# Fused Fourier mixing and MLP on one core: lighter warm-up products, a new first pair of products, and rows, weights and sums taken in another order

## The chip, the core and the metric

The kernel runs on one core of a Trainium2 chip. Its time is the device time of one execution in microseconds (us); the median of three runs of the kernel before is 850.76 us (850.23 to 850.90). Engines are named as the profile names them: PE (matrix products; PEld is its weight load), DVE (vector), ACT (scalar functions), POOL (GpSimd), SP (here a queue that only issues DMAs). POOL and ACT issue DMAs as well.

## What is computed

For x of 2048 rows and 640 columns:

```python
xn = layernorm(x)                       # no scale, no shift
a = xn @ dft_hid_re.T ; b = xn @ dft_hid_im.T
y = dft_seq_re @ a - dft_seq_im @ b     # Fourier mixing, real part
h = gelu_tanh(xn @ w1 + b1)             # 640 -> 1536
out = x + y + h @ w2 + b2               # 1536 -> 640
```

Everything is float32. The inputs hold the four DFT matrices in full (two of 2048 by 2048, two of 640 by 640).

## The kernel before

**Arithmetic.** A float32 operand is kept as a pair: a high part (written by ACT as a copy rounded to fp32r) and a low part (DVE: operand minus high part). A product of two operands is three PE instructions, high by high, high by low, low by high (`product`, L278 to L280; in the first MLP layer L304). `split` (L160 and L161) makes a pair. Nearly all PE instructions have 128 by 128 weights and 512 moving columns.

**Stages.** The 2048 rows are four blocks t of 512. Blocks 0 and 1 go through the MLP as written: iteration i of 12 takes 128 hidden units, and is one `hidden` (15 products), one `gelu` and one `output` (15 products into five banks). Blocks 2 and 3 are computed with fewer products from sums and differences of blocks and weights (`head`, `mid`, `finish`). Then come the two Fourier products, from 190 us on, which the change doesn't touch.

**The front (0 to 21 us).** Block 0 is four chunks of 128 rows. SP and ACT load one chunk each in turn. Before the rows arrive, PE runs ten products of zeros into a bank (`warm_up`, L676); their operand is a 128 by 512 tile that DVE clears (L665) and casts (L667). DVE (L185, L705) or ACT (L699 for the sum, L716) centers each chunk, PE transposes it by products with an identity matrix (`transpose_x`, L693, float32, 128 columns each), and `split` makes the pairs XT[j] from the five banks. W1[0] is split in two parts (L728, L729). Then `hidden(0)` and `hidden(1)` (L304) run as two blocks of 15, and `hidden(2)` follows, with four transposes (L764) after its first product. Scaling by the row's deviation is applied later (RB).

**Block 1's iterations (t = 1, i = 0 to 11, 95 to 178 us).** The program order of one iteration is: `hidden(g+2)`, `gelu(g+2)`, `output(g)`, `second_block(i)`, then `prep_w` of one step. So the pair `hs` that `gelu` makes in iteration i (ACT L322, ACT L326, DVE L328) is used by PE in iteration i+2. `second_block(i)` prepares blocks 2 and 3: mean and variance of chunks 12 to 15 (`ln_stats`, L185), their scaling (`ln_scale`, L192 to L197, with a change of ACT's function table; `ln_apply`, L201) and writing back to DRAM (`xs`, 16 DMAs, eight on POOL, eight on SP, L203), then reading block 2 and block 3 back turned by rows (`load_z`, L234) and turning them on DVE (`turn_z2`, `turn_z1`, L786 and L792). One buffer ("zo") holds, one after the other, block 0's result, block 2's rows, block 3's rows and block 1's input.

`prep_w` makes the weight pairs of the two 640 by 640 DFT matrices (wr and wi). Step s is column group j = s // 3 and part k = s % 3: k = 0 turns two raw tiles on DVE (L396) and loads the next two, and each part splits what it makes into regions of one staging tile `wst` and sends them to DRAM (`wits`, L418, POOL's queue). A region is written again only after its DMA has landed, and ACT, which runs its instructions in order, waits there with everything behind it.

**The end of block 1 (172 to 191 us).** `outs` and `outs_at` add the bias on ACT (L368), transpose a bank on DVE (L371) and add the rows on POOL (L373). `forms_ob` (sums of rows, the split of w1's sums TW[1], and one form) stands between two of them. A product that opens a bank (in `head(1)`: banks 5 and 6) waits until DVE has transposed what the bank held.

Queues run in program order; there is no scheduler. Tiles of one place wait for each other by tile.

Of the kernel before, what the change touches and what calls it, by code (L numbers as in the profile page):

```python
# [15 lines left out]
P = 128  # L16
Q = 4
B = 32
EPS = 1e-5
NWARM = 10  # L20
TAIL = 4
# [5 lines left out]
def kernel(  # L27
# [78 lines left out]
    def bank(k):  # L106
        return banks[:, k]
# [179 lines left out]
    def unit(g):  # L287
        return g if g < NF else LATE[g % NF]

    def hidden(g, aside=None):  # L290
# [4 lines left out]
        if g == 0:  # L295
            steps = FIRST
        if g == 1:

            steps.sort(key=lambda s: s[1] == 2)
        for n, (j, k) in enumerate(steps):  # L300
            if aside and n == ASIDE:
                aside()
            a, b = kinds[k]
            nc.tensor.matmul(  # L304
                acc, W1[i][:, a, j * P : (j + 1) * P], XT[j][:, b], start=n == 0, stop=n == len(steps) - 1
            )
        return acc


    FIRST = [(0, 0), (0, 2), (1, 0), (1, 2), (0, 1), (2, 0), (2, 2), (1, 1), (3, 0), (3, 2)]  # L310
    FIRST += [(2, 1), (4, 0), (4, 2), (3, 1), (4, 1)]

# [351 lines left out]
    make_identity(nc, ident)  # L664
    nc.vector.memset(zeros, 0.0)  # L665
    warm = whole["as"][:, :TB]
    nc.vector.tensor_copy(warm, zeros)  # L667

    nc.scalar.activation(eps[:, 1:2], eps[:, 0:1], AF.Sqrt)
    load_w1(0, cuts=(0, 2, ND))  # L670
    load_w1(1, cuts=(0, 2, ND))

    wacc = bank(0)

    def warm_up():
        nc.tensor.matmul(wacc, warm[:, :P], warm, start=True, stop=True)  # L676

    for k in range(NWARM):
        warm_up()
    load_w1(2)  # L680
    load_w2(0)
# [39 lines left out]
    ln_stats(2)  # L721
    center(2, ALU.subtract, MV[:, 2, 0:1])
    sum_on_act(3)
    center(3, ALU.add, MV[:, 3, 5:6], 0, 2)
    center(3, ALU.add, MV[:, 3, 5:6], 2, ND)
    for lo, hi in ((0, 2 * P), (2 * P, D)):
        h, l = (W1[0][:, k, lo:hi] for k in range(2))
        nc.scalar.activation(h, first_w1[:, lo:hi], AF.Copy)  # L728
        nc.vector.tensor_tensor(l, first_w1[:, lo:hi], h.bitcast(F32), op=ALU.subtract)  # L729
    transpose_x(0, 0, ND)  # L730
# [11 lines left out]
    acc0 = hidden(0)  # L742
    prep_w1(1)
    acc1 = hidden(1)

# [59 lines left out]
    def sums_w1(q):  # L805
# [7 lines left out]
        add(r[:, 2:4, :P], r[:, 2:4, :P], r[:, 2:4, P:], ALU.subtract)  # L813

    def split_w1(q):
        if q >= NF // 2:
            return
        TW[q] = A["tw"].tile([P, 2, 8 * P], F32R, tag=f"tw{q % 2}", bufs=1, name=f"tw{q}")
        split(TW[q][:, 0], TW[q][:, 1], RQ.pop(q).rearrange("p a b -> p (a b)"))
        TW[q] = TW[q].rearrange("p a (c f) -> p a c f", c=4)  # L820
# [149 lines left out]
    def open_tw():  # L970
        A["es"].close()
        A["w"] = None
        A["es"] = ExitStack()
        A["tw"] = pool("twp", stack=A["es"])

    def open_xf():
        es_rows.close()
        A["esx"] = ExitStack()
        A["xf"] = pool("xfp", side="right", stack=A["esx"])
        A["xfx"] = A["xf"].tile([P, 2, 2, TB], F32R, name="xfx")  # L980
        A["fifth"] = A["xf"].tile([P, TB], F32, name="fifth")
        load_rq(0)
# [66 lines left out]

    w_early = {0: (0,), 1: (1,), 2: (2,), 3: (3,), 4: (4,), 5: (5,)}  # L1050
    prep_w1(3)
    gelu(1, acc1)
    for g in range(NG):
# [37 lines left out]
        elif i < NF - 2:  # L1091
# [3 lines left out]
            second_block(i)  # L1095
            for k in w_early.get(i, ()):
                prep_w(k)
        elif i == NF - 2:
# [43 lines left out]

    outs(1, (0,), yt=lambda n: AB[:, 0], done=False)
    forms_ob()
    outs_at((2, 1), (4, 5))
    mid(0, rest)
# [659 lines left out]
```

## Time and profile before

| | us |
|---|---|
| median of three runs | 850.76 |
| the profiled execution: its own time | 853.42 |
| the profiled execution: span from the first to the last instruction | 851.6 |
| PE busy in the span | 842.5 |
| DVE, ACT, POOL busy in the span | 668.0, 355.3, 53.6 |
| first product of the first layer starts | 9.66 |

How to read it: PE is busy for 99% of the span, so what counts is where it isn't fed, and the share of any other engine over the whole span says little. A matmul's recorded duration (389 ns for 512 columns) is longer than the distance between two of them (227 ns), so a gap between two starts tells more than idle time. In a row of the timeline stand the start, the duration, the engine, the line, the operation, out<-in, the shapes and the count; in brackets stands the idle time before it and what ended it.

### The profile page before, as it was taken

The page shows a single profiled execution, that of the slowest core. Times are in us where ns is not written, and L with a number is a line of the kernel's source. Part 1 is how long each engine was busy: PE and PEld are TensorE (multiplying, and loading weights), DVE is VectorE, ACT ScalarE, POOL GpSimd, SP SyncE. Part 2 cuts the span into 40 slices and gives each one's busy share as a digit, 9 for nine tenths or more (in the row PEclk, how much of TensorE's full clock was granted, in tenths as well). Part 3 has the DMA queues.
Part 4 walks back from the last instruction along what each step waited for, and adds up shares of the span by engine and source line. Part 5 has one row for each costly group of instructions (what it writes and reads, how often), then busy time and mean ns, then how long its engine had stood idle before and what let it go on. Part 6 is the DMA issues. An engine that isn't in the chain of part 4 may idle for free.

```text
span 851.6 us, 10345 instructions
## 1 busy us (share of the span) xinstructions
PE 842.5 (99%) x3707; PEld 694.5 (82%) x3707; DVE 668.0 (78%) x841; ACT 355.3 (42%) x499; POOL 53.6 (6%) x78
## 2 busy tenths in 40 slices
PE   8999999999999999999999999999999999999997
PEld 6888888778888888888888888888888888888886
DVE  6766764795757888879988787899977898885687
ACT  7454533555655554333434343232322423223241
POOL 0000313131221300000000000000000000000001
PEclk9999999999999999999999999999999999999999
DMA  6667799738669998948743669763865879805464
GB/s 185 187 185 186 162 215 252 196 79 195 207 216 347 360 218 158 188 102 204 164 137 95 177 211 285 171 139 97 213 164 171 253 184 228 312 18 179 124 170 108
DMA packets 207363, 158.45 MB, mean 186 GB/s; under 512 B 81040, under 2 KB 180880, under 8 KB 206800
## 3 DMA queue, kind: packets, MB, share of 16 engines
q1 hardware_dynamic: 198368, 134.59, 62.2%
q0 software_dynamic: 4400, 21.89, 6.5%
q10 hardware_dynamic: 4544, 1.31, 0.6%
q8 instruction: 29, 0.48, 0.2%
q14 instruction: 22, 0.18, 0.1%
HBM read 114.76 MB, written 42.99 MB: 185 GB/s over the span
## 4 chain that ended last, share of the span: by engine, by line
PE 83%; DVE 4%; DMA 4%; ACT 3%; issue 3%; SPq 2%; POOL 1%; ACTq 0%; POOLq 0%; DVEq 0%
PE banks L278 27%; PE banks L279 26%; PE banks L280 26%; PE banks L304 3%; DMA x<-in_A_x_dram 1%; DMA wit<-wst 1%; SPq L388 1%; DMA xs<-x 1%; ACT ab L322 1%; SPq L203 0%; SPq L178 0%; POOL wit L418 0%; DVE r L161 0%; ACT hs L326 0%; DVE tw L161 0%
## 5 line engine op out<-in xcount | busy, mean ns | idle before, releaser
L278 PE MATMUL banks<-as,xab 128*128 128x512 f32 x411 | 160.0, 389 | 0.6 <-DVE zs L371 0.6
L279 PE MATMUL banks<-as,xab 128*128 128x512 f32 x411 | 159.9, 389 | 0.0
L280 PE MATMUL banks<-as,xab 128*128 128x512 f32 x411 | 159.9, 389 | 0.0
L160 ACT ACTIVATE as<-r 128x1024 fp32r<-128x1024 f32 x80 | 85.0, 1062 | 177.9 <-PE banks L280 149.5
L161 DVE TENSOR_TENSOR as<-r,as 128x1024 fp32r<-128x1024 f32 x80 | 97.1, 1215 | 41.5 <-ACT as L160 41.5
L278 PEld LDWEIGHTS banks<-as,xab 128*128 128x128 f32 x411 | 77.2, 188 | 17.0 <-DVE zs L371 1.0
L279 PEld LDWEIGHTS banks<-as,xab 128*128 128x128 f32 x411 | 77.2, 188 | 16.0
L280 PEld LDWEIGHTS banks<-as,xab 128*128 128x128 f32 x411 | 77.2, 188 | 15.9
L278 PE MATMUL banks<-as,xc 128*128 128x512 f32 x224 | 87.1, 389 | 0.0
L279 PE MATMUL banks<-as,xc 128*128 128x512 f32 x224 | 87.1, 389 | 0.0
L280 PE MATMUL banks<-as,xc 128*128 128x512 f32 x224 | 87.1, 389 | 0.0
L160 ACT ACTIVATE as<-rt 128x1024 fp32r<-128x1024 f32 x32 | 34.0, 1063 | 70.5 <-PE banks L280 62.5
L304 PE MATMUL banks<-xtt,xab 128*128 128x512 f32 x240 | 57.2, 391 | 0.2 <-ACT xtt L160 0.2
L304 PEld LDWEIGHTS banks<-xtt,xab 128*128 128x128 f32 x240 | 44.7, 188 | 10.1 <-ACT xtt L160 0.6
L278 PEld LDWEIGHTS banks<-as,xc 128*128 128x128 f32 x224 | 42.1, 188 | 8.8
L280 PEld LDWEIGHTS banks<-as,xc 128*128 128x128 f32 x224 | 42.1, 188 | 8.7
L279 PEld LDWEIGHTS banks<-as,xc 128*128 128x128 f32 x224 | 42.0, 188 | 8.7
L161 DVE TENSOR_TENSOR as<-rt,as 128x1024 fp32r<-128x1024 f32 x32 | 38.8, 1211 | 5.3 <-ACT as L160 5.3
L160 ACT ACTIVATE as<-u 128x1024 fp32r<-128x1024 f32 (+1 forms) x24 | 22.1, 919 | 48.2 <-PE banks L280 48.2
L512 DVE STREAM_TRANSPOSE r<-raw 128x1024 f32<-128x1024 f32 x32 | 39.5, 1239 | 3.0 <-PE banks L280 2.4
L161 DVE TENSOR_TENSOR as<-u,as 128x1024 fp32r<-128x1024 f32 (+1 forms) x24 | 24.9, 1041 | 18.8 <-ACT as L160 18.8
L512 DVE STREAM_TRANSPOSE rt<-raw 128x1024 f32<-128x1024 f32 x32 | 38.8, 1229 | 0.9 <-PE banks L280 0.8
(353 smaller groups left out, 1622.9 us busy)
## 6 DMA issues: line engine op xcount, KB each, us to landing
raw<-in_A_dft_seq_re_dram SPq DMA_DIRECT2D x64, 256.0 KB, 5.5
raw<-in_A_dft_seq_im_dram SPq DMA_DIRECT2D x64, 256.0 KB, 5.1
ws<-wit SPq DMA_DIRECT2D x15, 384.0 KB, 5.8
xo<-in_A_x_dram SPq DMA_DIRECT2D x16, 320.0 KB, 5.9
xab<-wit SPq DMA_DIRECT2D x13, 384.0 KB, 4.0
wit<-wstp POOLq DMA_DIRECT2D x12, 384.0 KB, 3.7
x<-in_A_x_dram SPq DMA_DIRECT2D x14, 320.0 KB, 4.4
xs<-x SPq DMA_DIRECT2D x56, 80.0 KB, 1.8
```

Source lines behind the costliest of these rows:

```text
L160: nc.scalar.activation(h, s, AF.Copy)
L161: nc.vector.tensor_tensor(l, s, h.bitcast(F32), op=ALU.subtract)
L278: nc.tensor.matmul(acc, wh, mh, start=first, stop=False, skip_group_check=goes_on)
L279: nc.tensor.matmul(acc, wh, ml, start=False, stop=False, skip_group_check=goes_on)
L280: nc.tensor.matmul(acc, wl, mh, start=False, stop=last, skip_group_check=goes_on)
L304: nc.tensor.matmul(acc, W1[i][:, a, j * P : (j + 1) * P], XT[j][:, b], start=n == 0, stop=n == len(steps) - 1)
L322: nc.scalar.activation(a, acc, AF.Gelu_apprx_tanh, bias=b1c[:, i : i + 1])
L388: nc.sync.dma_start(t[q * B : (q + 1) * B], v[:, :, s0 : s0 + B])
L512: nc.vector.transpose(held(pieces[g][2], u).rearrange("p c (n i) -> p c n i", i=B), r.rearrange("p n (c i) -> p c n i", i=B))
```

## The change

Front: `NWARM` goes from 10 to 13, and a warm-up product has 128 moving columns of plain float32 in place of 512 of fp32r; the cast goes, and the cleared tile is a quarter as wide. ACT centers the first two column groups of chunk 3 (128 rows by 256), DVE the other three; chunk 2 is centered in two parts. The split of W1[0]'s second part moves behind the first two splits of XT, the other three splits of XT and the split of W1[1] move into the new `first_two`, which runs the 30 products of `hidden(0)` and `hidden(1)` in one mixed order, with three transposes of chunk 3 after the second product. w1's second column block is loaded in four DMAs in place of eight, the third in eight in place of four.

```diff
-NWARM = 10
+NWARM = 13
...
+    def first_two():
+        kinds = ((0, 0), (0, 1), (1, 0))
+        second = sorted(((j, k) for j in range(ND) for k in range(3)), key=lambda s: s[1])
+        order = [(0, s) for s in FIRST[:13]] + [(1, s) for s in second[:2]]
+        order += [(0, FIRST[13]), (1, second[2]), (0, FIRST[14])] + [(1, s) for s in second[3:]]
+        for n, (g, (j, k)) in enumerate(order):
+            if n == 2:
+                transpose_x(3, 2, ND)
+                for e in range(2, ND):
+                    split(XT[e][:, 0], XT[e][:, 1], tacc[e])
+                prep_w1(1)
+            a, b = kinds[k]
+            ends = FIRST if g == 0 else second
+            nc.tensor.matmul(bank(g), W1[g][:, a, j * P : (j + 1) * P], XT[j][:, b],
...
-    FIRST = [(0, 0), (0, 2), (1, 0), (1, 2), (0, 1), (2, 0), (2, 2), (1, 1), (3, 0), (3, 2)]
-    FIRST += [(2, 1), (4, 0), (4, 2), (3, 1), (4, 1)]
+    FIRST = [(0, 0), (0, 2), (1, 0), (1, 2), (0, 1), (2, 0), (1, 1), (3, 0), (2, 2), (3, 2)]
+    FIRST += [(4, 0), (4, 2), (2, 1), (3, 1), (4, 1)]
...
-    nc.vector.memset(zeros, 0.0)
-    warm = whole["as"][:, :TB]
-    nc.vector.tensor_copy(warm, zeros)
+    nc.vector.memset(zeros[:, :P], 0.0)
...
-    load_w1(1, cuts=(0, 2, ND))
+    load_w1(1)
...
-        nc.tensor.matmul(wacc, warm[:, :P], warm, start=True, stop=True)
+        nc.tensor.matmul(wacc[:, :P], zeros[:, :P], zeros[:, :P], start=True, stop=True)
...
-    load_w1(2)
+    load_w1(2, cuts=(0, 2, ND))
...
-    center(2, ALU.subtract, MV[:, 2, 0:1])
     sum_on_act(3)
-    center(3, ALU.add, MV[:, 3, 5:6], 0, 2)
-    center(3, ALU.add, MV[:, 3, 5:6], 2, ND)
...
+    nc.scalar.activation(
+        chunked(xp[:, 3])[:, :, :2],
+        xt[3].rearrange("p (q c i) -> p q c i", q=Q, i=B)[:, :, :2],
+        AF.Identity,
+        bias=MV[:, 3, 5:6],
+    )
+    center(2, ALU.subtract, MV[:, 2, 0:1], 0, 2)
+    center(2, ALU.subtract, MV[:, 2, 0:1], 2, ND)
+    split_first(0, 2 * P)
+    center(3, ALU.add, MV[:, 3, 5:6], 2, ND)
...
-    for j0, j1 in ((0, 2), (2, ND)):
-        transpose_x(2, j0, j1)
-        transpose_x(3, j0, j1)
-    for j in range(ND):
+    transpose_x(2, 0, 1)
+    transpose_x(3, 0, 2)
+    transpose_x(2, 1, ND)
+    for j in range(2):
         split(XT[j][:, 0], XT[j][:, 1], tacc[j])
+    split_first(2 * P, D)
```

Block 1's iterations: statistics, scaling and writing of chunks 12 to 15 all move to iteration 0, ahead of `load_z(2)` and of `prep_w(0)`; block 3's rows are turned in iteration 5, not 6, and the loads that follow that (w1's first sums' rows `rq`, block 1's input `xo`) go with it; `prep_w` steps 3, 4 and 5 move one iteration later. The tile for w1's second sums takes its place first, over `wst`, and the one for the first sums goes behind it.

```diff
+        new_tw(1)
...
     def second_block(i):
         if i == 0:
-            load_z(2)
-            ln_stats(12)
-            ln_stats(13)
-        if i == 1:
-            ln_stats(14)
-            ln_stats(15)
-        if i == 2:
+            for c in range(12, 16):
+                ln_stats(c)
             ln_scale(12, 4)
             for c in range(12, 16):
                 ln_apply(c, nc.gpsimd if c < 14 else nc.sync)
+            load_z(2)
...
-        if i == 6:
-            form_of("a12", 0, two(2)[:, 0], lane("xc23", 2))
             turn_z2(ZT, 2)
             turn_z2(two(4), 0)
             turn_z1(A["zs"][:, 6 * TB : 7 * TB], 4)
+            load_rq(0)
             load_xo(1)
+        if i == 6:
+            form_of("a12", 0, two(2)[:, 0], lane("xc23", 2))
+            prep_w(5)
             open_tw()
...
-    w_early = {0: (0,), 1: (1,), 2: (2,), 3: (3,), 4: (4,), 5: (5,)}
+    w_early = {0: 0, 1: 1, 2: 2, 4: 3, 5: 4}
...
     outs(1, (0,), yt=lambda n: AB[:, 0], done=False)
+    outs_at((2,), (4,))
     forms_ob()
-    outs_at((2, 1), (4, 5))
+    outs_at((1,), (5,))
     mid(0, rest)
```

Three places show what this does to the order on an engine. The first is PE's queue from its start to the first products of the first layer (`xp` are centered rows, `xtt` the pairs XT, `xab_122` and `xab_123` W1's places). Before:

```order
L676 MATMUL banks<-as 128x512 x10
L693 MATMUL banks<-ident,xp 128x128 x10
L676 MATMUL banks<-as 128x512
L693 MATMUL banks<-ident,xp 128x128 x10
L304 MATMUL banks<-xtt,xab_122 128x512 x30
```

and of the change:

```order
L692 MATMUL banks<-zeros 128x128 x13
L709 MATMUL banks<-ident,xp 128x128 x10
L692 MATMUL banks<-zeros 128x128
L709 MATMUL banks<-ident,xp 128x128 x7
L304 MATMUL banks<-xtt,xab_122 128x512 x2
L709 MATMUL banks<-ident,xp 128x128 x3
L304 MATMUL banks<-xtt,xab_122 128x512 x28
```

Two products now stand ahead of the last three transposes. The second place is ACT's queue in iterations 3 to 5 of block 1 (`ab` and `hs` are `gelu`; `wst<-wt` is `prep_w`; `as` and `xc` are forms of block 2). Before, from iteration 3's `gelu`:

```order
L322 ACTIVATE ab<-banks,b1c 128x512
L326 ACTIVATE hs<-ab 128x512
L160 ACTIVATE wst<-wt_1_1217 128x256
L160 ACTIVATE wst<-wt_1_1217 128x128
L160 ACTIVATE wst<-wt_1_1219 128x256
L160 ACTIVATE wst<-wt_1_1219 128x128
L322 ACTIVATE ab<-banks,b1c 128x512
L326 ACTIVATE hs<-ab 128x512
L160 ACTIVATE as<-zs 128x512
```

and of the change, from the same `gelu`:

```order
L340 ACTIVATE ab<-banks,b1c 128x512
L344 ACTIVATE hs<-ab 128x512
L340 ACTIVATE ab<-banks,b1c 128x512
L344 ACTIVATE hs<-ab 128x512
L160 ACTIVATE as<-zs 128x512
L160 ACTIVATE wst<-wt_1_1261 128x256
L160 ACTIVATE wst<-wt_1_1261 128x128
L160 ACTIVATE wst<-wt_1_1263 128x256
L160 ACTIVATE wst<-wt_1_1263 128x128
```

Iteration 4's `gelu` no longer stands behind the splits of the second column group. The third place is DVE's queue at the end of block 1 (`ab<-banks` and `zs<-banks` are transposed banks, `tw` the split of w1's second sums, `hs<-zs` the form of `forms_ob`). Before:

```order
L371 STREAM_TRANSPOSE ab<-banks 128x512
L452 TENSOR_TENSOR zs<-zs,zt 128x1024
L161 TENSOR_TENSOR tw_1567<-rq_1424,tw_1567 128x1024
L161 TENSOR_TENSOR hs<-zs,hs 128x512
L371 STREAM_TRANSPOSE zs<-banks 128x512 x4
L452 TENSOR_TENSOR banks<-banks,fifth 128x512 x2
```

and of the change:

```order
L389 STREAM_TRANSPOSE ab<-banks 128x512
L389 STREAM_TRANSPOSE zs<-banks 128x512
L470 TENSOR_TENSOR zs<-zs,zt 128x1024
L161 TENSOR_TENSOR tw_1388<-rq_1428,tw_1388 128x1024
L161 TENSOR_TENSOR hs<-zs,hs 128x512
L389 STREAM_TRANSPOSE zs<-banks 128x512 x3
L470 TENSOR_TENSOR banks<-banks,fifth 128x512 x2
```

The transposition of bank 5 now stands ahead of the sum, the split and the form.

More of the change, by code (lines that the diff above doesn't have):

```diff
@@ L288, in unit @@
         return g if g < NF else LATE[g % NF]
+    def first_two():
[11 more added lines that the diff above has]
+            ends = FIRST if g == 0 else second
+            nc.tensor.matmul(
+                bank(g),
+                W1[g][:, a, j * P : (j + 1) * P],
+                XT[j][:, b],
+                start=(j, k) == ends[0],
+                stop=(j, k) == ends[-1],
+            )
+        return bank(0), bank(1)
     def hidden(g, aside=None):
@@ L294, in hidden @@
         steps = [(j, k) for j in range(ND) for k in range(3)]
[L295 to L299, printed above, removed]
         for n, (j, k) in enumerate(steps):
@@ L721, with split_first @@
     ln_stats(2)
-    center(2, ALU.subtract, MV[:, 2, 0:1])
     sum_on_act(3)
-    center(3, ALU.add, MV[:, 3, 5:6], 0, 2)
-    center(3, ALU.add, MV[:, 3, 5:6], 2, ND)
-    for lo, hi in ((0, 2 * P), (2 * P, D)):
+    def split_first(lo, hi):
         h, l = (W1[0][:, k, lo:hi] for k in range(2))
@@ L729 @@
         nc.vector.tensor_tensor(l, first_w1[:, lo:hi], h.bitcast(F32), op=ALU.subtract)
+    nc.scalar.activation(
[3 more added lines that the diff above has]
+        bias=MV[:, 3, 5:6],
+    )
+    center(2, ALU.subtract, MV[:, 2, 0:1], 0, 2)
+    center(2, ALU.subtract, MV[:, 2, 0:1], 2, ND)
+    split_first(0, 2 * P)
+    center(3, ALU.add, MV[:, 3, 5:6], 2, ND)
     transpose_x(0, 0, ND)
@@ L741 @@
         nc.sync.dma_start(b2c[q * B : (q + 1) * B], b2[q * DQ : (q + 1) * DQ].rearrange("(c i) -> i c", i=B))
-    acc0 = hidden(0)
-    prep_w1(1)
-    acc1 = hidden(1)
+    acc0, acc1 = first_two()
     nc.gpsimd.tensor_scalar(MV[:, 1::2, 0], MV[:, 1::2, 5], -1.0, None, op0=ALU.mult)
@@ L813, in sums_w1, with new_tw @@
         add(r[:, 2:4, :P], r[:, 2:4, :P], r[:, 2:4, P:], ALU.subtract)
+    def new_tw(q):
+        TW[q] = A["tw"].tile([P, 2, 8 * P], F32R, tag=f"tw{q % 2}", bufs=1, name=f"tw{q}")
     def split_w1(q):
@@ L817, in split_w1 @@
             return
-        TW[q] = A["tw"].tile([P, 2, 8 * P], F32R, tag=f"tw{q % 2}", bufs=1, name=f"tw{q}")
+        if q != 1:
+            new_tw(q)
         split(TW[q][:, 0], TW[q][:, 1], RQ.pop(q).rearrange("p a b -> p (a b)"))
@@ L981, in open_xf @@
         A["fifth"] = A["xf"].tile([P, TB], F32, name="fifth")
-        load_rq(0)
     def second_block(i):
         if i == 0:
-            load_z(2)
-            ln_stats(12)
-            ln_stats(13)
-        if i == 1:
-            ln_stats(14)
-            ln_stats(15)
-        if i == 2:
+            for c in range(12, 16):
+                ln_stats(c)
             ln_scale(12, 4)
@@ L1095 @@
             second_block(i)
-            for k in w_early.get(i, ()):
-                prep_w(k)
+            if i in w_early:
+                prep_w(w_early[i])
         elif i == NF - 2:
```

## Prediction

> **What bounds the kernel now.** I read the page first, then PE's timeline, then that of the engines it waited for.
>
> ```profile
> span 851.6 us, 10345 instructions
> PE 842.5 (99%) x3707; PEld 694.5 (82%) x3707; DVE 668.0 (78%) x841; ACT 355.3 (42%) x499; POOL 53.6 (6%) x78
> ```
>
> PE is the bound nearly everywhere: a gain can only come from an earlier first product or from the few places where PE isn't fed. The idle times in brackets lie between modelled ends; the true loss is the distance between starts. These are PE's starts in block 1's iterations 6, 7, 8, 9 (each begins with the 15 L304 products) and at the end of block 1.
>
> ```profile
> 139.70 3.56 PE L304 MATMUL banks<-xtt,as 128*128 128x512 f32 x15
> ...
> 146.87 3.56 PE L304 MATMUL banks<-xtt,as 128*128 128x512 f32 x15
> 150.83 0.49 PE L278 MATMUL banks<-hs,r 128*128 128x512 f32 x1 [0.39 <-ACT hs L326]
> 151.91 0.50 PE L279 MATMUL banks<-hs,r 128*128 128x512 f32 x1 [0.58 <-DVE hs L328]
> ...
> 155.21 3.56 PE L304 MATMUL banks<-xtt,xab 128*128 128x512 f32 x15
> ...
> 162.01 1.30 PE L304 MATMUL banks<-xtt,xab 128*128 128x512 f32 x5
> ```
> ```profile
> 182.87 0.39 PE L280 MATMUL banks<-xtt,tw 128*128 128x512 f32 x1
> 183.83 0.50 PE L278 MATMUL banks<-as,xab 128*128 128x512 f32 x1 [0.58 <-DVE zs L371]
> 184.17 0.40 PE L279 MATMUL banks<-as,xab 128*128 128x512 f32 x1
> ...
> 186.82 0.50 PE L278 MATMUL banks<-r,tw 128*128 128x512 f32 x1
> ```
>
> An iteration without a wait is 155.21 to 162.01, 6.80 us for 30 products, 0.227 each. Iteration 6 took 7.17 and iteration 7 took 8.34: 0.37 and 1.54 lost, **1.91 in all**. At the end of block 1 the step 182.87 to 183.83 is 0.96, and the restart behind it 0.34, so 0.85 is lost; from 184.17 to 186.82 eleven steps took 2.65 and not 2.50, and another restart follows: 0.25. About **1.1** there.
>
> **The front.** The timeline to the first products:
>
> ```profile
> 1.91 4.46 PE L676 MATMUL banks<-as 128*128 128x512 f32 x10 [1.91 <-DVE as L667]
> 6.39 1.28 PE L693 MATMUL banks<-ident,xp 128*128 128x128 f32 x10
> 6.57 0.74 ACT L699 ACTIVATE ab<-x 128x640 f32<-128x640 f32 x1 [0.18 <-DMA x<-in_A_x_dram]
> ...
> 7.44 1.20 DVE L705 TENSOR_SCALAR xp<-x,mv 128x640 f32<-128x640 f32 x3
> ...
> 8.59 0.52 ACT L728 ACTIVATE xab<-w1r 128x384 fp32r<-128x384 f32 x1 [0.85 <-DMA w1r<-in_B_w_dram]
> 9.02 2.53 ACT L160 ACTIVATE xtt<-banks 128x512 fp32r<-128x512 f32 x5
> ...
> 9.66 7.54 PE L304 MATMUL banks<-xtt,xab 128*128 128x512 f32 x31 [0.20 <-ACT xtt L160]
> ```
>
> ACT's first XT split starts at 9.02, behind W1[0]'s second part, which sat 0.85 idle for its DMA; PE starts 0.05 after the split's 0.58. In the change ACT ends the sum of chunk 3 at 7.4 as before, then centers 256 columns (not in this trace; 384 columns of L728 took 0.52, 640 of L699 0.74, so some 0.42, with 0.74 as the upper end), then splits W1[0]'s first part, 256 columns as well: 8.2 to 8.5. The transposes it needs, one of chunk 2 and one of chunk 3, hang on the same centering (7.9 to 8.2, and 0.3 for the product to end), so XT's split runs 8.3 to 8.9 and the first product starts at 8.95, at the late end 9.25: 0.4 to 0.7 earlier. Three float32 transposes now stand between the products (0.11 each by L693's ten in 1.28, and 0.1 restart: 0.45). The 31 products before took 7.54 less 0.39 for the last one's duration, 7.15 for 30 steps, where 30 times 0.227 is 6.80; some 0.1 of that 0.35 is the start, which stays, and 0.25 can go, since W1[1] has four larger DMAs and is wanted later. DVE's work for the second product (W1[0]'s low part, done at 8.7) and for the three transposes (chunk 3's other three groups, 0.41 more, 9.1) is early enough. Sum 0.6 - 0.45 + 0.25: **0.4 gained**, between 0.1 and 0.65. The shorter clear and the missing cast gain nothing themselves: the warm-up is covered by the row DMAs, which end at 6.57. If that cover goes, PE's first transposes slip with it.
>
> **Iterations 0 to 7.** `hs` made in iteration i is due 17.0 us after iteration i's first product (15 + 30 + 30 products), so at 122.7 for i = 1, then every 6.8. Why it came late:
>
> ```profile
> 140.88 0.62 ACT L160 ACTIVATE wst<-wt 128x256 fp32r<-128x256 f32 x2 [2.37 <-DVE wt L396]
> ...
> 148.92 0.62 ACT L160 ACTIVATE wst<-wt 128x256 fp32r<-128x256 f32 x2 [1.58 <-DMA wit<-wst]
> ```
> ```profile
> x<-in_A_x_dram SPq DMA_DIRECT2D x14, 320.0 KB, 4.4
> ```
> ```profile
> 102.41 2.38 SPq L178 DMA_DIRECT2D x<-in_A_x_dram  x4
> ```
> ```profile
> 124.08 0.68 DVE L328 TENSOR_TENSOR hs<-ab,hs 128x512 fp32r<-128x512 f32 x1
> ...
> 126.16 2.18 DVE L201 TENSOR_SCALAR x<-x,mv 128x640 f32<-128x640 f32 x4
> ...
> 133.57 0.69 DVE L328 TENSOR_TENSOR hs<-ab,hs 128x512 fp32r<-128x512 f32 x1 [2.24 <-ACT hs L326]
> ```
> ```profile
> 130.89 1.28 ACT L322 ACT_TABLE_LOAD   x1
> ```
> ```profile
> 116.46 1.32 POOL L418 DMA_DIRECT2D wit<-wst  x2 [11.80 <-DVE wst L161]
> ...
> 127.07 4.30 POOL L203 DMA_DIRECT2D xs<-x  x8 [3.32 <-DVE x L201]
> ```
>
> ACT's next work after the first row is iteration 4's `gelu`, after the second iteration 5's: one stood behind the second column group, the other behind the landing of its weights. In the change iteration 4's `gelu` follows iteration 3's directly, 7 us early; 5's and 6's get the waits of steps 3 and 4, with a deadline 6.8 later. From the same durations I get `hs` of iterations 5, 6 and 7 some 4 to 5 us before they are due. So 1.91 goes.
>
> What is late next is iteration 2's and 3's `hs`: POOL's eight `xs` issues (4.30) now stand ahead of the first `wit` pair, and ACT's table change, DVE's four scalings ahead of the first turn. Chunk 15's load lands near 109.2 (issued by 104.79, 4.4 by the page); with about 1.1 for its statistics and 1.5 for the deviations the four scalings (2.18) start near 112 and POOL's issues near 113, so POOL is free near 117.4 and the first `wit` goes out 1.0 later than 116.46. Its landing shares the DMA engines with 1.3 MB of `xs` that used to go from 127 on: nothing to 4.9 us more (at the 265 GB/s of 116 to 118, in the view by windows below). Iteration 2's `hs` ended at 124.8 and is due at 129.5, iteration 3's at 134.3, of which 1.3 is a table load that is now gone, and due at 136.3. With the middle, 3.5 later, both just make it; with the far end, 5.9, PE loses up to 2.6 here. I take nothing lost.
>
> ```profile
> 116.00:118.00 2.00, 2.00 (x11) 1.65 (x10) 1.39 (x5) 1.51 (x4) 1.32 (x2) 1.00 1.19 265
> 180.00:190.00 10.00, 9.42 (x41) 6.94 (x39) 10.00 (x12) 4.07 (x8) 6.97 (x5) 1.00 0.44 117
> ```
>
> **The end of block 1.** From 180 to 190 DVE, the third busy time, is busy 10.00 of 10.00: PE gains there only as far as DVE is ahead. These rows of DVE (and one of POOL) set it:
>
> ```profile
> 155.15 1.27 DVE L161 TENSOR_TENSOR wst<-wt,wst 128x256 fp32r<-128x256 f32 x3 [2.10 <-ACT wst L160]
> ...
> 158.45 1.24 DVE L786 STREAM_TRANSPOSE zt<-z 128x1024 f32<-128x1024 f32 x1
> ...
> 160.74 0.67 DVE L792 STREAM_TRANSPOSE zs<-z 128x512 f32<-128x512 f32 x1
> 161.33 0.65 DVE L328 TENSOR_TENSOR hs<-ab,hs 128x512 fp32r<-128x512 f32 x1
> ...
> 164.63 1.23 DVE L161 TENSOR_TENSOR tw<-rq,tw 128x1024 fp32r<-128x1024 f32 x1 [1.13 <-ACT tw L160]
> ...
> 180.24 2.31 DVE L161 TENSOR_TENSOR tw<-rq,tw 128x1024 fp32r<-128x1024 f32 x1
> ...
> 183.08 2.50 DVE L371 STREAM_TRANSPOSE zs<-banks 128x512 f32<-128x512 f32 x4
> 185.50 1.26 DVE L452 TENSOR_TENSOR banks<-banks,fifth 128x512 f32<-128x512 f32 x2
> ```
> ```profile
> 179.35 2.12 POOL L373 TENSOR_TENSOR xo<-xo,ab 128x512 f32<-128x512 f32 x1 [21.88 <-DVE ab L371]
> ```
>
> The three turns (2.96 from 158.45 to 161.41) leave this stretch, step 5's three splits (1.27) stay in it, but wait for nothing that is later. So w1's first sums start near 158 instead of 161.9, and DVE runs 1.7 (turns less splits) to 3.9 earlier from there on. PE comes 0.4 + 1.91 = 2.3 earlier. Bank 5's transposition moves ahead of the sum, the split of 2.31 and the form, so the 0.85 at 182.87 goes at any of these. Then the additions of L452 are last: done at 186.76, needed for PE's step at 186.82, which without the 0.85 and with 2.3 comes at 183.5. With DVE 3.0 earlier they end at 183.8: 0.4 with the restart is lost again. **0.7 of the 1.1 is gained**, 0 to 1.1.
>
> One row speaks against this order: the split took 2.31 beside POOL's addition (179.35 to 181.47) and 1.23 alone. The change gives POOL a second addition right before the split. The Trainium skill (SBUF — State Buffer, SBUF: two separate sides) says that a DVE operation with two SBUF inputs and a GpSimd operation that reads SBUF lock each other out for a whole instruction. By that rule the split waits for both additions, about 1.3 more by the row; the trace agrees as to one addition (181.47 + 1.23 is 182.7, it ended at 182.55).
>
> **Sum.** 0.4 + 1.9 + 0.7 = 3.0. Nothing from 190 on is changed, and PE has no long gap there, so the gain should stay: the profiled execution 853.4 would come to 850.4. It lies 2.7 above the median of the runs (850.76), from which I take the same 3.0: **847.8**.
>
> **The rivals.**
> *The wait moves on to DVE.* PE reaches the end of block 1 2.3 earlier, but DVE's chain only the 1.7 of the turns, and all after it moves by 1.7: 849.1. For it speaks the 10.00 of 10.00, and the doubled additions; against it that DVE had waits in that chain (1.13 for ACT) which can shrink. The rule on the port would lead here too.
>
> *The rows crowd out the weights (slower).* Place: iterations 1 to 3. The landings of `wit` follow each other (a region is split again after the first landed, and sent again), so a delay can come twice: 1.0 + 2 times 4.9 is 10.8, iteration 3's `hs` at 143.8 against 136.3, 7.5 lost, less the 3.0 gained: 855.3 at worst, 852.9 in the middle of that (5.1 lost). It is slower than before if that `hs` comes after 139.3. Against it: the same bytes are then missing from 127 on, where the second landings fall.
>
> *The clock isn't up.* The first ten products cost 0.43 each, twice the later 0.227, so the warm-up is needed. Of the light product the trace shows no price: a quarter of 0.43 by its columns, 0.11, up to the same 0.43. L693's float32 products of 128 columns cost 0.11 where 512 fp32r columns cost 0.227, double by column; at half rate 0.22, 13 of them end at 4.1 and PE idles 2.2 us before the first transposes. If that holds the clock down until 4 us (1.91 to about 6 before) after 6.39, the transposes and some three products run at half rate: 0.9 up to the first product and 1.2 behind it, 849.9. The Trainium skill (FP8 and Floating Point Precision, TensorE Precision Notes) says that true float32 takes four passes; by it 13 products cost 13 times 0.43 and end at about 6.7, no idle time is left, and the sum stays; no row here shows it.
>
> **How the numbers follow.** Forecast 847.8 with its own range of 847.0 to 848.9: 0.60. Wait moves on, 849.1 (848.5 to 850): 0.22. Clock, 849.9: 0.09. Rows crowd out weights, 850 to 855: 0.09. The range of 846.9 to 850.0 holds all but some 0.15. Runs of this kernel can tell 0.2%, 1.7 us: faster is below 849.06. That holds for the forecast, for half of the first rival and little of the second: 0.73; the same 0.20; slower, above 852.46, the larger part of the crowding: 0.07.
>
> **What would show it.** The first L304 near 9.0 and the 31st near 16.4 (9.66 and 16.81 now); light products 0.43 apart until 6 us. Iterations of 6.80 throughout from 98.9 to the end of block 1, and no ACT wait in front of iterations 4 and 5's `gelu`. No wait of PE for L389; at most one of some 0.3 for the additions (now L470). The forecast is wrong if an L278 waits for `hs` near 129 or 136, if PE's gap at the opening of `finish` grows to 1 us, or if new gaps show behind 190.

## The result and the profile after

The change makes the kernel **slower**: 857.9 us (median of six runs, 855.58 to 859.1) against 850.73; the ratio is 1.008, with a 95% interval of 1.0067 to 1.0094. The prediction was 847.8. The profiled execution of the change took 858.04 with a span of 856.3.

PE's waits in the changed kernel, by what it waited for (us in total, times, longest; L340 to L346 are now `gelu`, L389 the transposition of a bank at the end of block 1, L885 a copy of a bank by ACT, L322 the first layer):

```profile
PE banks L278 <- DVE zs L389: 2.1, 1, 2.1
PE banks L278 <- ACT hs L344: 1.7, 3, 0.9
...
PE banks L279 <- DVE hs L346: 1.0, 3, 0.6
```

Two views of PE's timeline show where these stand: the 31st product of the first layer, and block 1 from 139 us on.

```profile
16.34 0.39 PE L322 MATMUL banks<-xtt,xab 128*128 128x512 f32 x1
```
```profile
139.24 3.56 PE L322 MATMUL banks<-xtt,as 128*128 128x512 f32 x15
146.06 3.56 PE L322 MATMUL banks<-xtt,as 128*128 128x512 f32 x15
152.86 3.56 PE L322 MATMUL banks<-xtt,xab 128*128 128x512 f32 x15
156.63 0.50 PE L278 MATMUL banks<-hs,r 128*128 128x512 f32 x1 [0.20 <-ACT hs L344]
157.71 0.50 PE L279 MATMUL banks<-hs,r 128*128 128x512 f32 x1 [0.58 <-DVE hs L346]
161.02 3.56 PE L322 MATMUL banks<-xtt,xab 128*128 128x512 f32 x15
165.21 0.49 PE L278 MATMUL banks<-hs,rt 128*128 128x512 f32 x1 [0.63 <-ACT hs L344]
...
170.31 0.49 PE L278 MATMUL banks<-hs,rt 128*128 128x512 f32 x1 [0.87 <-ACT hs L344]
...
184.61 0.50 PE L278 MATMUL banks<-xtt,tw 128*128 128x512 f32 x1 [0.59 <-ACT banks L885]
...
186.10 0.39 PE L278 MATMUL banks<-as,xab 128*128 128x512 f32 x1
...
189.73 0.50 PE L278 MATMUL banks<-r,tw 128*128 128x512 f32 x1 [2.10 <-DVE zs L389]
```

In this execution the front does what it should: the 31st product starts at 16.34 and not 16.81, and the iterations that start at 139 and 146 us take 6.8 and start 0.5 and 0.8 earlier than in the first profile of before. Then `hs` is late three times, near 156, 164 and 169 us; by distances between starts that is 1.32, 1.40 and 1.64. The first is for the `hs` of iteration 6, the others for those of 7 and 8. At the end of block 1 the step before 184.61 loses 0.86 and the one before 189.73, which opens bank 6, 2.38, plus 0.28 behind it. Bank 5's opening, the row of 186.10, does not wait. In sum PE loses 8.2 from 142 to 192 us, where the first profile of before lost 3.3. Behind 192 us the two hardly differ: the two executions are 4.6 apart (858.04 and 853.42), which is these 4.9 less the front's head start of some 0.5.

ACT and DVE in that place show what `hs` waited for. ACT first (`wst<-wt` are splits of wr and wi), then DVE, then DVE's turn of block 2 in the first profile of before:

```profile
153.09 0.42 ACT L160 ACTIVATE wst<-wt 128x256 fp32r<-128x256 f32 x1 [5.47 <-DMA wit<-wst]
...
154.72 0.62 ACT L160 ACTIVATE wst<-wt 128x256 fp32r<-128x256 f32 x2 [1.01 <-DVE wt L470]
155.24 0.67 ACT L340 ACTIVATE ab<-banks,b1c 128x512 f32<-128x512 f32 x1
```
```profile
139.06 2.37 DVE L810 STREAM_TRANSPOSE zs<-z 128x1024 f32<-128x1024 f32 x2 [5.12 <-DMA z<-xs]
...
150.87 1.25 DVE L810 STREAM_TRANSPOSE zt<-z 128x1024 f32<-128x1024 f32 x1 [2.36 <-DMA z<-xs]
...
153.17 0.67 DVE L816 STREAM_TRANSPOSE zs<-z 128x512 f32<-128x512 f32 x1
153.76 0.38 DVE L161 TENSOR_TENSOR wst<-wt,wst 128x256 fp32r<-128x256 f32 x1
```
```profile
134.18 2.37 DVE L786 STREAM_TRANSPOSE zs<-z 128x1024 f32<-128x1024 f32 x2
```

Two waits end at nearly the same time. ACT stands 5.47 until the weights of step 3 have landed (their splits ran 4 us later than before, since block 2 was turned at 139.06 and not at 134.18). DVE stands 2.36 until block 3 has landed, turns it, and only then does the low halves of step 4, which ACT's second column group of that step waits for. The next `gelu` stands behind both.

Where the delay of what comes from DRAM begins is seen on SP's queue (first the change, then before):

```profile
118.81 8.18 SPq L203 DMA_DIRECT2D xs<-x  x8
127.04 3.15 SPq L234 DMA_DIRECT2D z<-xs  x4
130.30 8.91 SPq L406 DMA_DIRECT2D wraw<-in_A_dft_hid_re_dram  x4
```
```profile
121.59 2.16 SPq L234 DMA_DIRECT2D z<-xs  x4
124.18 6.97 SPq L388 DMA_DIRECT2D wraw<-in_A_dft_hid_re_dram  x4
```

The rows go out first and hold SP until 127; block 2's reading starts 5.4 later, and the next raw weights 6.1. The DMA engines leave little room to catch up (busy time by windows, the last two columns are the share of the 16 DMA engines and GB/s; of the change, then of before):

```profile
116.00:122.00 6.00, 6.00 (x28) 4.96 (x27) 3.40 (x8) 3.84 (x7) 4.05 (x9) 1.00 1.13 257
...
134.00:140.00 6.00, 6.00 (x28) 4.96 (x27) 0.94 (x1) 0.46 (x1) 0.00 (x0) 1.00 1.09 256
```
```profile
116.00:122.00 6.00, 6.00 (x28) 4.97 (x27) 4.58 (x14) 2.29 (x7) 1.86 (x3) 1.00 0.99 259
...
128.00:134.00 6.00, 6.00 (x28) 4.98 (x27) 1.91 (x5) 3.02 (x4) 4.50 (x10) 1.00 1.12 291
```

The share is near or above 1 in these windows in both kernels (in the change it is 0.85 from 122 to 128): what goes earlier puts something else later. No run separates SP's order from the full DMA engines as the reason for the 5.4.

### The profile page after: what moved, and what is told of

Same layout as the page of the kernel before. It is cut to its first block, busy times and chain, and to the rows that moved or that the text cites. A ratio compares the mean times of both kernels' runs of the same rounds, so it can differ in the third digit from the quotient of the medians.

```text
span 856.3 us, 10377 instructions
## 1 busy us (share of the span) xinstructions
PE 843.5 (99%) x3724; PEld 695.5 (81%) x3724; DVE 666.7 (78%) x840; ACT 356.2 (42%) x500; POOL 54.0 (6%) x78
## 4 chain that ended last, share of the span: by engine, by line
PE 83%; DVE 5%; issue 5%; DMA 4%; ACT 2%; SPq 1%; POOL 1%; DVEq 0%; POOLq 0%; ACTq 0%
PE banks L278 26%; PE banks L279 26%; PE banks L280 26%; PE banks L322 2%; DMA x<-in_A_x_dram 1%; DMA z<-xs 1%; DMA wit<-wst 1%; PE banks L304 1%; DVE st L185 1%; DMA xs<-x 1%; POOL wit L436 0%; SPq L203 0%; ACT ab L340 0%; DVE xtt L161 0%; DVE r L161 0%
## 5 line engine op out<-in xcount | busy, mean ns | idle before, releaser
L322 PE MATMUL banks<-xtt,xab 128*128 128x512 f32 x210 | 50.0, 390 | 0.0
L322 PEld LDWEIGHTS banks<-xtt,xab 128*128 128x128 f32 x210 | 39.3, 188 | 8.2
```

The source lines that it names most:

```text
L322: nc.tensor.matmul(acc, W1[i][:, a, j * P : (j + 1) * P], XT[j][:, b], start=n == 0, stop=n == len(steps) - 1)
```

## The experiments

Each was timed in five rounds beside the kernel before, except the second profile of that kernel. Times are medians; the ratio is to the runs of before on the same chip. The theory I started with was that the early rows are the cause (ROWS); the rivals were the later steps of wr and wi, block 3's turn, and the order at the end.

**Before, profiled again** (nothing edited).

> The kernel before, unchanged, profiled again. Its profiled execution took 853.4 where its other runs took 850.2 to 850.9. If 853.4 was a single late execution, this one is 850 to 851, its losses for hs near 150 us and at 183 to 187 us are about 2.7 us smaller than the 3.0 that the first profile shows, and that gain was never there to be had; if the profile always adds 2.7, this one is near 853.4 with the same losses.

It took 851.32, while the other runs beside it had a median of 850.37. Its first product starts at 10.17, 0.5 later than in the first profile. Yet PE's timeline has no bracket at all in iterations 6 to 9, and each is 6.80:

```profile
140.40 3.56 PE L304 MATMUL banks<-xtt,as 128*128 128x512 f32 x15
147.20 3.56 PE L304 MATMUL banks<-xtt,as 128*128 128x512 f32 x15
...
160.80 3.56 PE L304 MATMUL banks<-xtt,xab 128*128 128x512 f32 x15
```

By distances between starts it loses 0.3 from 142 to 192 us, where the first profile lost 3.3. So the 1.91 in iterations 6 and 7 and most of the 1.1 at the end belonged to the one execution that was profiled first. These 3.0, less the 0.7 by which the first execution was earlier at the 31st product, are about the 2.1 between the two executions (853.42 and 851.32). That the other runs near 850.4 have no such losses either is likely by their time; they were not profiled.

**The front alone.** The front's part of the diff on the kernel before.

> Before, with only the front of the change (lighter warm-up products, ACT's centering, the first two blocks mixed, w1's loads cut otherwise). All theories: PE is 0.46 us ahead from 17 us on as in the change, the stalls of iterations 6 and 7 (1.91 us) and at the end of block 1 (1.1) are those of before, so about 850.3 us, ratio 0.9995. If the front disturbs the transfers of block 1 (rival: x loads 1 us later because of it), the stalls near 150 and 164 grow and it is slower than before, up to 855.

852.6 us, ratio 1.0025 (1.0016 to 1.0034): a miss. In its profile the first product is at 9.01, and PE then waits for `hs` near 137, 144, 151 and 158 us (0.1 to 0.65 each by distances between starts) and 1.57 at the opening of bank 5. Near 31 us it loses 0.85, for a split of w1. Two of these rows on its timeline:

```profile
151.52 0.50 PE L279 MATMUL banks<-hs,r 128*128 128x512 f32 x1 [0.38 <-DVE hs L346]
184.60 0.50 PE L278 MATMUL banks<-as,xab 128*128 128x512 f32 x1 [1.30 <-DVE zs L389]
```

In this execution an earlier PE finds the chain of transfers, ACT and DVE where it was or later, and loses more than it had gained. But it is the slowest of the eleven (854.14), so these losses are larger than those of the median, and may in part be its own, as in the first profile of before.

**The front alone, w1's loads cut as before.**

```diff
-    load_w1(1)
+    load_w1(1, cuts=(0, 2, ND))
...
-    load_w1(2, cuts=(0, 2, ND))
+    load_w1(2)
```

> The front alone (852.6 for 0.7 earlier first products), with the loads of w1's second and third block cut as before. Theory CUTS (other cuts make w1's fourth block land up to 1.3 us late, which stops PE for 0.85 at 30 us in the front's profile): that stop goes, 851 or less (1.001). Theory CHAIN (PE comes earlier to hs, whose weights land when they land, and the early PE only waits there): the time stays, 852 to 853 (1.002 to 1.003).

853.25, ratio 1.0026 (1.0016 to 1.0037). The stop at 30 us is gone from this profile, but one of 0.83 has come at 13.37, for the split of w1's second block; the time stays. CUTS falls. (This profile, too, is of the slowest run, 854.22.)

**The rows written where they were.** `second_block(0)` to `(2)` of before in the changed kernel.

> The change, with the statistics, scaling and writing of chunks 12 to 15 and load_z(2) where they were before (iterations 0 to 2). Theory ROWS (the early writing holds up the first wit pair, the reading of block 2 and with it everything DVE and ACT do later): the three stalls for hs at 156, 164 and 169 us (1.32, 1.40, 1.64) go, and half or more of the 2.4 at 187; 852 us or less (ratio 1.002 or less). Theory WEIGHTS (steps 3 to 5 of wr and wi one iteration later are the cause): they stay, 857 to 858 (1.007 or more). Theory TURN (block 3's turn, rq and xo in iteration 5 are the cause): they stay as well.

859.32, ratio 1.0106 (1.009 to 1.0121). **ROWS as the only cause falls**: the stalls at 156, 164 and 169 are there to 0.1 us. But all that leads up to them is 5 us earlier, and then DVE stands. On SP's queue block 3's reading, and on DVE's timeline its turn:

```profile
140.63 2.69 SPq L234 DMA_DIRECT2D z<-xs  x4
```
```profile
150.82 1.25 DVE L810 STREAM_TRANSPOSE zt<-z 128x1024 f32<-128x1024 f32 x1 [7.26 <-DMA z<-xs]
```

Block 3 lands at 150.7 in both. Its reading needs its rows in DRAM and the buffer that block 2 leaves. With early rows the buffer is late (turned by 142.03, first DMA at 142.06); with late rows the rows are (last landed at 140.54, first DMA at 140.63). Writing the rows earlier does not bring block 3 earlier.

**Block 3's turn where it was.**

```diff
         if i == 5:
...
-            turn_z2(ZT, 2)
-            turn_z2(two(4), 0)
-            turn_z1(A["zs"][:, 6 * TB : 7 * TB], 4)
-            load_rq(0)
-            load_xo(1)
         if i == 6:
             form_of("a12", 0, two(2)[:, 0], lane("xc23", 2))
+            turn_z2(ZT, 2)
+            turn_z2(two(4), 0)
+            turn_z1(A["zs"][:, 6 * TB : 7 * TB], 4)
+            load_xo(1)
...
         A["fifth"] = A["xf"].tile([P, TB], F32, name="fifth")
+        load_rq(0)
```

> The change, with block 3's turn and the loads of rq and xo in iteration 6 (rq in iteration 4) as before; the early rows stay. In the change two things end at nearly the same time ahead of step 4's splits: block 3's landing (150.75, turned by 153.8 on DVE) and the landing of step 3's first weights (153.01, 8 us later than it is with the rows written later). Theory TWO CHAINS: taking away one leaves the other: the stall near 156 us stays (about 1.3), those near 164 and 169 (3.0) shrink since the weights no longer land beside xo's load; 855 to 856.5 (1.005 to 1.007). Theory TURN ALONE: all three go, 853 or less (1.003). Theory ROWS ALONE has fallen already.

854.43, ratio 1.0043 (1.003 to 1.0055). The stalls for `hs` are gone but for 0.28 at 157, where TWO CHAINS had 1.3: for `hs` TURN ALONE is nearer, and the weights of step 3, still late, hold nobody up once DVE does not stand. What is left is at the end of block 1 (0.77 at 180.6, 2.26 at 185.7 and 1.4 of half clock behind that, below), where DVE is late with the early rows too.

**Both undone.**

> Both undone: rows where they were, and block 3's turn in iteration 6. What is left of the change is the front, the three later steps of wr and wi, the order at the end of block 1 and w1's tiles. Theory TWO CHAINS: no stall for hs from 122 to 178 us, 2 us or less at the end of block 1; 849 to 851.5 (0.999 to 1.001). Theory that the later steps of wr and wi cost by themselves: stalls for hs near 164 and 171 remain, 854 or more (1.004).

850.74, ratio 1.0002 (0.9993 to 1.0011), as expected of two causes. No PE wait for `hs` is left; block 3's turn now finds its rows after 0.98. The later steps of wr and wi do not cost by themselves here.

**Steps 3 to 5 of wr and wi where they were.**

```diff
-    w_early = {0: 0, 1: 1, 2: 2, 4: 3, 5: 4}
+    w_early = {0: 0, 1: 1, 2: 2, 3: 3, 4: 4, 5: 5}
...
-            prep_w(5)
```

> The change, with prep_w steps 3, 4, 5 in iterations 3, 4, 5 as before. Theory WEIGHTS: the stalls for hs at 156, 164 and 169 go, 853.5 us (1.003). Theory ROWS: gelu of iterations 4 and 5 stands again behind splits whose staging is later than before, so the stalls come earlier and sum to at least as much: 858 or more (1.008 or more).

857.97, ratio 1.0092 (1.0077 to 1.0106), at the edge of what ROWS said. The wait moves forward to iteration 6, for the `hs` of iteration 4, and is larger:

```profile
145.82 0.50 PE L278 MATMUL banks<-hs,r 128*128 128x512 f32 x1 [2.69 <-ACT hs L344]
```

The time is that of the change (857.9): with the rows and the turn early, the later steps move the wait and neither win nor lose.

**xo's load behind step 5.** `load_xo(1)` moved behind `prep_w(5)` in iteration 6.

> The change, with xo's load (block 1's input, 153.9 to 163.3) issued in iteration 6 behind step 5 of wr and wi; the turn stays in iteration 5. Theory TRAFFIC (the weights' landing of 7.4 us beside that load is what makes hs late at 164 and 169): those stalls (3.0) fall below 0.7 and DVE comes earlier at the end; 854.5 or less (1.0045). Theory DVE WAIT (DVE standing until block 3 has landed, with step 4's splits behind it, is enough): they stay, 857 to 858.

858.46, ratio 1.0091 (1.0077 to 1.0105). The run did not do what I meant: nothing else stands on SP's queue there, so the load went out at 152.8, as soon as the buffer was free. Whether its traffic adds to the delay stays open. The run with the front and the later steps (below) has xo's load at the same place beside the weights of step 5 and loses nothing (its queues of SP and of POOL):

```profile
155.09 1.98 SPq L381 DMA_DIRECT2D xo<-in_A_x_dram  x4
```
```profile
155.66 1.60 POOL L436 DMA_DIRECT2D wit<-wst  x3 [7.65 <-DVE wst L161]
```

**The order at the end of block 1 as before.**

```diff
-    outs_at((2,), (4,))
     forms_ob()
-    outs_at((1,), (5,))
+    outs_at((2, 1), (4, 5))
```

> The change, with bank 5's transposition again behind the sum, the split and the form at the end of block 1. Theory END (this order costs by itself, the two additions of POOL beside the split): the 2.38 at 187 and 0.86 at 183.6 fall to the 1.1 of before, 855.8 (1.006). Theories ROWS, WEIGHTS, TURN: DVE is late there whatever the order, the time changes by less than 1 us, and PE waits at the opening of bank 5 instead: 857 to 859 (1.007 to 1.010).

856.73, ratio 1.0071 (1.0057 to 1.0085), 1.2 less than the change, though the intervals overlap. In its profile the opening of bank 5 waits again (1.71 by distances, at 187.58) and bank 6 does not: at the end of block 1 PE loses 3.0 in place of 3.7. DVE and then POOL in the change, and DVE with the order of before:

```profile
183.63 1.98 DVE L470 TENSOR_TENSOR zs<-zs,zt 128x1024 f32<-128x1024 f32 x1
185.53 2.32 DVE L161 TENSOR_TENSOR tw<-rq,tw 128x1024 fp32r<-128x1024 f32 x1
```
```profile
183.25 1.28 POOL L391 TENSOR_TENSOR xo<-xo,ab 128x512 f32<-128x512 f32 x1 [17.89 <-DVE ab L389]
184.49 2.27 POOL L391 TENSOR_TENSOR xo<-xo,zs 128x512 f32<-128x512 f32 x1
```
```profile
182.90 1.18 DVE L470 TENSOR_TENSOR zs<-zs,zt 128x1024 f32<-128x1024 f32 x1
184.00 2.29 DVE L161 TENSOR_TENSOR tw<-rq,tw 128x1024 fp32r<-128x1024 f32 x1
```

The second addition costs DVE 0.8 on the sum. The ends alternate: addition 184.53, sum 185.61, addition 186.76, split 187.85, each 1.1 to 1.2 behind the one before, about what each takes alone (1.18 for the sum, 1.23 for the split, some 1.3 for an addition). That is what the Trainium skill (SBUF — State Buffer, SBUF: two separate sides) says of a DVE operation with two SBUF inputs and a GpSimd operation that reads SBUF: the pair of ports is held for a whole instruction, and the other waits. This trace agrees.

**The front, the later steps and w1's tiles alone.** Rows, turn and end order of before.

> The front and the three later steps of wr and wi alone: rows, block 3's turn and the order at the end of block 1 are those of before. Against the run with only the end still changed (850.74, 0.89 lost at 182 to 185 us). Theory END COSTS (bank 5 transposed early puts a second addition of POOL beside DVE's sum): the loss at the end falls to 0.3, 850.1 (0.9996). Theory END PAYS as I predicted: it grows by 0.5, 851.2 (1.001).

850.03, ratio 0.9997 (0.9988 to 1.0007). No PE wait from 120 to 190 us above 0.11. END COSTS is favoured: 0.7 less than with the end's new order, though the intervals overlap.

**The same with the early rows.**

> The front, the early rows and the three later steps; block 3's turn and the order at the end of block 1 are those of before. The same without the end undone took 854.43 and lost 0.66 at 180 and 2.26 at 184 us, with half clock behind that. Theory END COSTS: most of that goes, 851.5 to 852.5 (1.0015 to 1.0025), and what is left over the kernel before is the price of the early rows. Theory DVE LATE (the early rows make DVE late at the end whatever its order): PE waits at another place there, 853.5 to 854.5.

853.59, ratio 1.0039 (1.0026 to 1.0052): 3.6 above the last run, on the same chip. **That is the price of the early rows.** The end's new order adds only 0.8 to it (854.43; the intervals overlap), so DVE LATE was nearer. PE waits where the rival of the prediction had it, for one `hs` near 157, and at the end:

```profile
129.75 0.50 PE L279 MATMUL banks<-hs,xc 128*128 128x512 f32 x1 [0.35 <-DVE hs L346]
...
157.80 0.50 PE L279 MATMUL banks<-hs,r 128*128 128x512 f32 x1 [0.55 <-DVE hs L346]
...
181.53 0.50 PE L278 MATMUL banks<-xtt,tw 128*128 128x512 f32 x1 [0.52 <-ACT banks L885]
184.63 0.50 PE L278 MATMUL banks<-as,xab 128*128 128x512 f32 x1 [1.44 <-DVE zs L389]
```

**The later steps alone, on the kernel before.** `w_early` of the change, `prep_w(5)` in iteration 6.

> The kernel before, with only steps 3, 4 and 5 of wr and wi one iteration later. The second profile of before has no stall for hs in iterations 6 and 7, so there is nothing for the later steps to win in a usual execution: 850.2 to 850.6 (1.000). If the first profile's 1.91 are usual, 848.8 (0.998). With the front on top of it (the other run of this call) 0.5 less, if the front's gain is kept once hs is early enough; the same, if it is lost elsewhere.

852.68, ratio 1.0025 (1.0015 to 1.0036): a miss. The profile is of the slowest of its eight runs (854.36), but the next experiment tests what it shows. The split of w1's first sums goes to the place of the staging tile, whose last weights now land at 164.5:

```profile
164.76 1.06 ACT L160 ACTIVATE tw<-rq 128x1024 fp32r<-128x1024 f32 x1 [8.54 <-DMA xo<-in_A_x_dram]
```

(The releaser named is not the one: xo is not an operand here; the last transfer from the staging tile ended 0.2 earlier.)

**The later steps with the exchange of w1's tiles.**

```diff
         A["tw"] = pool("twp", stack=A["es"])
+        new_tw(1)
...
-        TW[q] = A["tw"].tile([P, 2, 8 * P], F32R, tag=f"tw{q % 2}", bufs=1, name=f"tw{q}")
+        if q != 1:
+            new_tw(q)
```

> The kernel before with the three later steps of wr and wi and with w1's first sums moved off the staging tile (the run with the later steps alone, 852.68, lost 1.47 at 167 us since that split waited 8.5 us for the last weights to leave the staging tile, and 2.5 at 181 to 185 behind it). Theory EXCHANGE: both losses go, and what is left is before's usual time with no stall, 849.8 to 850.5. Theory CHAIN AT THE FRONT'S COST: without the front PE starts 0.7 later, so it is 0.5 above the front with these steps (850.03): 850.5. If the front costs by itself as it did alone (2.2), it is 848.5 or less.

850.19, ratio 0.9998 (0.9989 to 1.0007): EXCHANGE holds, 2.5 less than without it.

**The same with the front, on the same chip.**

> The front with the later steps and w1's tiles once more, on the same chip as the same without the front: 850.0 (0.9995), so that the two give the front's own worth where hs is early: 0.5 by the first products (0.7 earlier, 0.45 of it left at 17 us), or nothing if it is lost behind.

850.23, ratio 0.9996 (0.9987 to 1.0005). The front is worth nothing that can be measured, even where no `hs` is late. The two profiles show one reason: the 31st product starts at 16.66 with the front and at 16.50 without, so here the front has no head start to lose. Over all profiles it starts at 16.21 to 16.67 in the eleven with the whole front, at 16.50 to 17.50 in the four without: the head start is some 0.4 in the middle, but single executions differ by as much.

Put in order, the times make a ladder from before to the change:

| | us | step |
|---|---|---|
| before (five groups of runs) | 850.33 to 850.73 | |
| front, later steps, w1's tiles | 850.03, 850.23 | 0 |
| and the rows early | 853.59 | +3.6 |
| and bank 5 transposed early | 854.43 | +0.8 |
| and block 3 turned in iteration 5 (the change) | 857.9 | +3.5 |

The +0.8 is not clear of the noise; the two others are. The steps depend on their order: with late rows the turn costs 8.6 (859.32 against 850.74). No version tried beats the kernel before by more than can be measured; 850.03 is the lowest.

## Why the prediction was wrong, point by point

- **What bounds the kernel.** PE is the bound, right. But 1.91 and 1.1 were read from one execution, and the step "from which I take the same 3.0" carried them over to the median. The text itself had the warning: the execution lay 2.7 above the median. The second profile has next to nothing of either (0.3). Without them at most the front's 0.4 was there to win.
- **The front, -0.4.** As worked out: first product at 8.99 (8.95 said), the 31st at 16.34 (16.4 said). But these are one execution each, and the start differs between executions by as much as the gain. In the times nothing of it is left: 0 beside the later steps, and the front alone is 2.2 slower.
- **The light products.** 0.43 each (two records, 0.213 apart) until the clock rises near 4.1 us, as the sentence on four passes had it, and not the 0.22 of the clock rival; then 0.22 (0.112 apart). So thirteen take 4.61 and not 13 times 0.43, PE is idle for 0.86 behind them, and the first product is not late. The row on PE's timeline is below. What the Trainium skill (FP8 and Floating Point Precision, TensorE Precision Notes) says of four passes fits both prices: 128 columns cost here what 512 columns of fp32r cost, 0.43 before the rise and 0.227 after it.

```profile
1.05 4.61 PE L692 MATMUL banks<-zeros 128*128 128x128 f32 x26 [1.05 <-DVE zeros L683]
```

- **"From the same durations I get `hs` of iterations 5, 6 and 7 some 4 to 5 us before they are due."** This step failed. It took the splits away from in front of `gelu` and left out what was put there: block 3's turn in iteration 5, in DVE's queue ahead of step 4's low halves. I counted the turns as 2.96 of DVE work that leaves the end, but not what they wait for. The `hs` of iteration 5 was in time (ended at 147.30, used from 149.46, so 2.2 early); those of 6, 7 and 8 were late. In place of 1.91 gained, 4.4 were lost at 156, 164 and 169; undoing the turn takes 3.5 off, and 8.6 when the rows are late.
- **"What is late next is iteration 2's and 3's `hs`" and nothing lost.** In the profile of the change nothing is lost there, as said; the early rows without the turn lose 0.6 at 129.75. But the delay was not over with these iterations: first weights 2.5 later (118.93 against 116.46; 1.0 said), block 2 turned 4.9 later, step 3's weights landing at 153.0. It came out five iterations on.
- **The end of block 1, -0.7.** Wrong in sign. DVE came some 4 us later, not 1.7 to 3.9 earlier, since `hs`, step 5 and w1's sums all hang on the two waits; the 0.85 at bank 5's opening did go, as forecast (186.10 has no wait), but PE now stands 0.86 for ACT's copy ahead of it and 2.38 at the opening of bank 6, which is transposed behind the split. The second addition fell on the sum as well as on the split. Undone, the order takes 1.2 off the change (0.7 by the waits of the two profiles; the intervals overlap).
- **The rivals.** "The rows crowd out the weights" named the cause of 3.6, with 852.9 for its middle where the version with the rows early and nothing else that costs measures 853.59. That is luck: its middle took 3.0 gained from 5.1 lost, and nothing was gained. It named only one of two causes, and at too early a place. It was given 0.09. "The wait moves on to DVE" is what the end shows, with a DVE that is late and not one that gains less.

**What stays open:** why the front alone, with nothing else changed, costs 2.2 (below is what its traces have in common), whether the early rows cost by SP's order or by the DMA engines' load, and how much xo's traffic adds.

## What to carry to other kernels

A stall is worth removing only if more than one execution has it: when the profiled execution lies above the median by about what you mean to win, profile again first. When an instruction moves ahead of others in an in-order queue, its own wait moves with it, so look up when its operand lands before counting the wait that it was moved away from. Where the DMA engines are full, an earlier transfer is a trade against the one that it displaces, and the bill can come many iterations later.

## What the runs showed of the hardware

**Half clock after short idle times.** After 2.10 idle at the end of block 1 (2.49 between two starts) the run with block 3's turn undone shows PE at half clock for 3.4 us (windows; the clock is the third column from the right):

```profile
183.60:185.70 2.10, 0.03 (x1) 0.00 (x0) 2.10 (x5) 0.00 (x0) 0.54 (x1) 0.98 0.32 88
185.70:189.00 3.30, 3.27 (x8) 2.59 (x9) 3.30 (x5) 0.84 (x2) 3.30 (x3) 0.50 0.82 213
```

The change itself had the same 2.10 and kept its clock:

```profile
189.80:193.00 3.20, 3.08 (x12) 2.21 (x13) 3.20 (x5) 1.18 (x2) 3.20 (x3) 1.00 0.84 216
```

Of the five profiles with such an idle time (2.08 to 2.69), three have such a stretch; it cost 1.4 here. The Trainium skill (TensorE: Matmul & The Clock Gate, Why this matters for your kernels) says that gaps above some 3 us bring it; here 2.1 sometimes did.

**A landing that depends on the front.** DVE's first turn of block 1's rows waits for their last landing; in before, and in the change (with its front 0.5 earlier):

```profile
78.60 0.71 DVE L238 STREAM_TRANSPOSE zt<-z 128x512 f32<-128x512 f32 x1 [0.47 <-DMA z<-xs]
```
```profile
79.61 0.71 DVE L238 STREAM_TRANSPOSE zt<-z 128x512 f32<-128x512 f32 x1 [1.93 <-DMA z<-xs]
```

In the four profiles without the front that wait is 0.47 to 0.64, in eleven of the twelve with it 1.56 to 2.01 (in the twelfth 0.29). So the chain of transfers behind it starts later although PE is earlier; what makes the landing late was not found.
